# DeltaNet and a gated feed-forward on one core: two ways of inverting the first two pairs of chunks, and a new order of work

## The chip, the cores and the metric

The kernel runs on one core of one Trainium2 chip. That core has a matrix engine (TensorE, PE in the profile, its weight loads PEld), a vector engine (VectorE, DVE), a scalar engine (ScalarE, ACT), a general engine (GpSimd, POOL) and a synchronising engine (SyncE, SP); SP and ACT issue most of the DMA transfers, each in the order of its own instructions. The metric is the device time of one execution in microseconds; the median of several runs counts.

## The reference

```python
    batch, n_heads, seq, head_dim = (4, 8, 768, 48)
...
    k_n = k / (np.linalg.norm(k, axis=-1, keepdims=True) + 1e-06)
    state = np.zeros((B, H, D, D), dtype=np.float32)
    for t in range(S):
        kt, vt, bt = (k_n[:, :, t], v[:, :, t], beta[:, :, t, None])
        y[:, :, t] = np.einsum('bhd,bhde->bhe', q[:, :, t], state)
        v_old = np.einsum('bhde,bhd->bhe', state, kt)
        state = state + bt[:, :, :, None] * np.einsum('bhd,bhe->bhde', kt, vt - v_old)
...
    n_tokens, d_model, d_ff = (3072, 384, 2048)
...
    h = x @ w_in
    g = h * np.cos(h)
    return (g @ w_out).astype(np.float32)
```

The recurrence runs over 768 steps for 4 x 8 heads. Its outputs, turned to 3072 rows of 384, go through the feed-forward with the gate h cos(h). The weights arrive as 64-bit floats and are narrowed to 32 bits on the chip.

## The kernel before

**Units and pairs.** The 768 steps are cut into 24 chunks of C = 32, called units (n). A unit holds all 32 heads: 4 batches of 32 steps lie on the 128 partitions, 8 heads along the free dimension. Two units make a pair (m = n // 2), and a pair is also one block p of 256 tokens of the feed-forward.

**One unit.** Keys and queries are turned (`turn`, on PE for units 0 to 7, later by DVE), and `gram` multiplies keys by keys and by queries. `gram_keys` scales the key part by beta and the squared norm; it is I + N with N strictly triangular, 32 x 32 for each head. The unit needs its inverse. With it, `solve` turns the right side (v less what the state gives, `right_side`) into the updates u; `update` and `update_out` add them to the state; `through_state` and `within` give the outputs; `within_out`, `features` and `features_out` turn them into the columns x of the feed-forward. Units follow one another through the state.

**The inversion before.** For a pair the Gram blocks of both units are written to HBM (`gram_put`) and read back (`gram_get`) so that each partition holds one head's matrix. `invert` then eliminates column by column: for column j a product (L735) and a subtraction (L742), each on all 128 partitions. The result goes to HBM (`put`) and comes back as blocks (`get`). Pairs 1 to 11 do so on POOL with 31 columns, two partitions to a matrix. Pair 0 (HALVED = 1) inverts only the two diagonal 16 x 16 halves, on DVE: `fold` packs them, 15 columns are eliminated in PSUM, and the unit is then solved in two steps with the off-diagonal quarter between them (`solve_half`, `half_out`, `between`, `between_out`, `solve`).

**The feed-forward.** Pairs 0 and 1 are computed plainly (`hidden`, eight blocks p_h <- x_ffn, w_in a pair, at L951), the others with a Strassen-like scheme on PE (`layer`, L1125) whose sums are formed on DVE and POOL. The output of pair 0 is plain (`output`, L1148), those of the others use seven products (`product`, L1205). A gate takes an ACT pass, a DVE pass, the sine on ACT and a product on DVE. Each of the 28 weight tiles (12 of w_in, 16 of w_out) is loaded into a buffer of the gates, split by ACT (L495, L497), shifted by DVE (L501, L506) and added up by POOL (L510).

**The order.** Nothing is scheduled while it runs. Every piece of work is a task with a key; `Order.LINE` lists the tasks by number in the order in which they are written out, and each engine, and each DMA queue, keeps that order. `Order.OTHER` names the tasks that go to the second of two engines (POOL in place of DVE, ACT's queue in place of SP's). So an instruction that waits holds up everything behind it on its engine.

Of the kernel before, what the change touches and what calls it, by code (L numbers as in the profile page):

```python
# [10 lines left out]
FP = mybir.dt.float32  # L11
# [5 lines left out]
C = 32  # L17
DP = 64
SPLIT = 2
# [27 lines left out]

class Order:

    OTHER = {  # L50
        ('gram_put', 0), ('put', 0), ('get', 1), ('k', 2), ('gram_put', 2), ('q', 3), ('v',
        3), ('gram_get', 1), ('k', 5), ('k', 6), ('gram_put', 6), ('get', 6), ('v', 7),
        ('gram_put', 7), ('blocks', 8, 1), ('blocks', 9, 1), ('gram_put', 9), ('blocks', 11,
        1), ('put', 5), ('get', 11), ('blocks', 12, 1), ('gram_put', 12), ('blocks', 13, 1),
        ('put', 6), ('get', 14), ('put', 7), ('v', 16), ('blocks', 16, 0), ('get', 17),
        ('k', 18), ('v', 18), ('put', 9), ('k', 20), ('gram_get', 10), ('gram_put', 22),
        ('blocks', 23, 1), ('store', 0, 1), ('right', 4, 4), ('right', 3, 4), ('left', 1, 1,
        1), ('left', 1, 4, 0), ('in_sums', 20), ('x_sum', 2, 'd'), ('x_sum', 2, 'n'),
        ('x_sum', 2, 'm'), ('x_sum', 2, 'e'), ('x_sum', 2, 'k'), ('x_sum', 2, 'g'),
        ('x_sum', 2, 'l'), ('x_sum', 2, 'f'), ('left', 2, 1, 0), ('left', 2, 2, 0), ('left',  # L60
        2, 4, 0), ('store', 2, 0), ('x_sum', 3, 'd'), ('x_sum', 3, 'n'), ('x_sum', 3, 'e'),
        ('x_sum', 3, 'k'), ('x_sum', 3, 'g'), ('x_sum', 3, 'i'), ('x_sum', 3, 'l'),
        ('x_sum', 3, 'f'), ('x_sum', 3, 'h'), ('x_sum', 3, 'b0'), ('left', 3, 2, 0),
        ('left', 3, 3, 0), ('x_sum', 4, 'd'), ('x_sum', 4, 'n'), ('x_sum', 4, 'm'),
        ('x_sum', 4, 'e'), ('x_sum', 4, 'g'), ('x_sum', 4, 'f'), ('x_sum', 4, 'h'),
        ('x_sum', 4, 'b0'), ('left', 4, 1, 0), ('left', 4, 2, 0), ('left', 4, 1, 1),
        ('store', 4, 1), ('x_sum', 5, 'd'), ('x_sum', 5, 'n'), ('x_sum', 5, 'm'), ('x_sum',
        5, 'i'), ('x_sum', 5, 'l'), ('left', 5, 1, 0), ('left', 5, 2, 0), ('left', 5, 1, 1),
# [155 lines left out]
def kernel(  # L224
# [199 lines left out]
    for t in half_tiles:  # L424
        nc.vector.memset(t, 0.0)
        off_blocks.extend((t[:, 0], t[:, 1]))
        half_zt.extend((t[:, 2], t[:, 3]))
# [1353 lines left out]
```

## Time and profile before

| what | us |
|---|---|
| median of 3 runs (648.1 to 654.56) | 652.11 |
| the profiled execution | 653.98 |
| its span, first to last instruction | 652.2 |
| PE busy in it | 593.1 |
| DVE busy | 505.0 |
| POOL busy | 458.3 |
| ACT busy | 295.2 |
| first `hidden` block starts at | 71.2 |

The span is the profiled execution without what lies around it. In the page, the forty digits of an engine are its busy share in forty equal slices of 16.3 us, in tenths. A group of instructions is given by line, engine, operation and tiles, then its busy time, the mean of one in ns, and the idle time ahead of it with what ended it. The chain of waits is followed back from the last instruction: start, length, and what it was.

### The profile page before, as it was taken

To read this page: it belongs to the slowest core of one execution; us is meant where nothing else is said; L and a number is where in the kernel's file an instruction comes from. 1 tells how busy PE (TensorE), PEld (TensorE's weight loads), DVE (VectorE), ACT (ScalarE), POOL (GpSimd) and SP (SyncE) were. 2 spreads that over 40 slices of the span, in tenths; PEclk is the share of its full clock that TensorE was granted. 3 is DMA by queue.
4 is the path that set the end of the run, shared out by engine and by line. 5 is a ranking of instruction groups with operands and counts; after the bars stand their busy time and mean duration, and the time that the engine had idled before them with its cause. 6 is when DMAs were issued, how large, how long until landed. Compare 5 with 4: busy or idle time off the path is not lost.

```text
span 652.2 us, 23408 instructions
## 1 busy us (share of the span) xinstructions
PE 593.1 (91%) x9784; PEld 554.9 (85%) x9784; DVE 505.0 (77%) x1035; ACT 295.2 (45%) x518; POOL 458.3 (70%) x813
## 2 busy tenths in 40 slices
PE   3305789999999999999999999999999999999997
PEld 3204689897889999999999999999898999999997
DVE  4684498889879987988879879889668779666582
ACT  2534366663234444535634535536334545545340
POOL 4368878978898778888788787658687388424130
PEclk9999999999999999999999999999999999999999
DMA  8886576362473363454443622441531400300001
GB/s 167 199 183 158 135 179 145 88 135 46 66 122 58 53 112 59 86 82 73 85 74 52 113 42 54 56 88 22 100 69 24 82 12 3 58 2 25 1 24 26
DMA packets 215809, 51.52 MB, mean 79 GB/s; under 512 B 207256, under 2 KB 210600, under 8 KB 215704
## 3 DMA queue, kind: packets, MB, share of 16 engines
q1 hardware_dynamic: 160324, 35.06, 28.3%
q10 hardware_dynamic: 55124, 14.53, 11.0%
q8 instruction: 77, 1.26, 0.8%
q0 software_dynamic: 256, 0.45, 0.3%
q14 instruction: 28, 0.23, 0.1%
HBM read 39.24 MB, written 10.75 MB: 77 GB/s over the span
## 4 chain that ended last, share of the span: by engine, by line
PE 72%; POOL 8%; DMA 7%; DVE 5%; issue 3%; ACTq 2%; SPq 1%; ACT 1%; POOLq 0%; DVEq 0%
PE p_out L1205 25%; PE p_h L1125 23%; PE p_h L951 7%; POOL part L735 3%; POOL z L742 3%; PE p_out L1148 3%; PE p_kq L795 3%; DMA kp<-in_k_dram 3%; PE p_s L892 2%; PE p_kq L909 2%; PE p_u L867 2%; DMA gb<-g_dr 2%; PE p_g L625 1%; PE p_h L1205 1%; PE p_z L930 1%
## 5 line engine op out<-in xcount | busy, mean ns | idle before, releaser
L735 POOL TENSOR_TENSOR part<-z,gb 128x126 f32<-128x126 f32 (+22 forms) x341 | 150.8, 442 | 53.1 <-ACT g_ffn L1137 9.0
L742 POOL TENSOR_TENSOR z<-z,part 128x126 f32<-128x126 f32 (+22 forms) x341 | 155.1, 455 | 26.7
L1205 PE MATMUL p_out<-w_out,g_ffn 128*128 128x192 f32 x672 | 121.6, 329 | 2.9 <-ACT o L1244 1.5
L1205 PEld LDWEIGHTS p_out<-w_out,g_ffn 128*128 128x128 f32 x672 | 107.8, 190 | 4.3 <-ACT o L1244 1.7
L1004 ACT ACTIVATE turns<-turns,halfpi 128x512 f32<-128x512 f32 x96 | 68.3, 720 | 82.5 <-DVE turns L995 68.0
L1205 PE MATMUL p_out<-w_sum,g_ffn 128*128 128x192 f32 x496 | 90.8, 330 | 0.0
L1125 PE MATMUL p_h<-x_sum,w_in 128*128 128x128 f32 x640 | 83.3, 278 | 0.8 <-ACT p_h L1137 0.8
L1205 PEld LDWEIGHTS p_out<-w_sum,g_ffn 128*128 128x128 f32 x496 | 79.4, 190 | 1.2 <-DVE o L1257 0.2
L1125 PEld LDWEIGHTS p_h<-x_sum,w_in 128*128 128x128 f32 x640 | 77.5, 191 | 2.5 <-issue 0.6
L988 ACT ACTIVATE turns<-g_ffn,quarter_turn 128x512 int32<-128x512 f32 x70 | 49.6, 719 | 49.9 <-DVE g_ffn L1142 18.3
L1142 DVE TENSOR_TENSOR g_ffn<-g_ffn,p_h 128x512 f32<-128x512 f32 x80 | 54.0, 680 | 16.8 <-PE p_h L1125 15.5
L1007 DVE TENSOR_TENSOR g_ffn<-turns,g_ffn 128x512 f32<-128x512 f32 x70 | 51.7, 746 | 13.4 <-ACT turns L1004 13.2
L922 ACT COPY y<-p_kq 32x384 f32<-32x384 f32 x96 | 45.2, 470 | 34.4 <-PE p_kq L909 29.2
L995 DVE SCALAR_TENSOR_TENSOR turns<-g_ffn,turns 128x512 f32<-128x512 f32 x70 | 55.3, 798 | 6.2 <-ACT turns L988 6.2
L1125 PE MATMUL p_h<-x_sum,in_sum 128*128 128x128 f32 x400 | 53.7, 278 | 1.0 <-ACT p_h L1137 0.8
L1125 PEld LDWEIGHTS p_h<-x_sum,in_sum 128*128 128x128 f32 x400 | 49.7, 191 | 2.2 <-ACT p_h L1137 1.1
L951 PE MATMUL p_h<-x_ffn,w_in 128*128 128x128 f32 x384 | 48.2, 285 | 0.0
L1221 POOL TENSOR_TENSOR g_ffn<-g_ffn 128x512 f32<-128x512 f32 x21 | 30.3, 1450 | 24.8 <-DVE g_ffn L1007 14.6
L544 POOL TENSOR_TENSOR knrm<-ksum,halves 128x16 f32<-128x16 f32 (+1 forms) x14 | 37.9, 2711 | 12.8 <-DVE ksum L532 12.5
L951 PEld LDWEIGHTS p_h<-x_ffn,w_in 128*128 128x128 f32 x384 | 46.0, 199 | 1.1 <-POOL z L742 0.2
L1257 DVE SCALAR_TENSOR_TENSOR o<-p_out,o 128x192 f32<-128x192 f32 x74 | 25.0, 350 | 26.9 <-PE p_out L1205 26.0
L1125 PE MATMUL p_h<-x_ffn,w_in 128*128 128x128 f32 x320 | 42.3, 276 | 0.0
(135 smaller groups left out, 1018.8 us busy)
## 6 DMA issues: line engine op xcount, KB each, us to landing
gb<-g_dr SPq DMA_DIRECT2D x18, 256.0 KB
g_ffn<-in_moe_w_out_dram SPq DMA_DIRECT2D x11, 384.0 KB
vp<-in_v_dram SPq DMA_DIRECT2D x80, 48.0 KB
g_ffn<-in_moe_w_in_dram SPq DMA_DIRECT2D x6, 512.0 KB
g_ffn<-in_moe_w_in_dram ACTq DMA_DIRECT2D x6, 512.0 KB
kp<-in_k_dram SPq DMA_DIRECT2D x112, 24.0 KB
out_dram<-o SPq DMA_DIRECT2D x13, 192.0 KB
zt<-z_dr SPq DMA_DIRECT2D x72, 32.0 KB
```

What stands on the lines that cost most here:

```text
L544: nc.gpsimd.tensor_tensor(out=scales[m][2][:, part], in0=sums[m, part.start][:, 0:n], in1=halves[:, 0:n], op=ALU.pow,)
L735: eng.tensor_tensor(out=part, in0=z[:, 0:rows, j, None].to_broadcast(shape), in1=a[:, j, None, j + 1 :].to_broadcast(shape), op=ALU.mult,)
L742: eng.tensor_tensor(out=behind, in0=behind, in1=part, op=ALU.subtract)
L922: nc.scalar.copy(by_parity(y[quarter(b)]), p_kq[quarter(b ^ 1), :, b % 2])
L951: nc.tensor.matmul(p_h[:, i], w_in[:, t, (4 * k + i) * 128 : (4 * k + i + 1) * 128], xts[p][:, t, unit * 128 : (unit + 1) * 128], start=(i ...
L988: nc.scalar.activation(turns[p, f], hidden_of(p, f), AF.Identity, bias=quarter_turn, scale=TURN)
L995: nc.vector.scalar_tensor_tensor(out=r, in0=hidden_of(p, f), scalar=TURN, in1=t, op0=ALU.mult, op1=ALU.subtract,)
L1004: nc.scalar.activation(r, r, AF.Sin, bias=halfpi, scale=2.0 * math.pi)
L1007: nc.vector.tensor_tensor(out=place(p, f), in0=step_of(rests.pop((p, f)), f), in1=step_of(hidden_of(p, f), f), op=ALU.mult,)
L1125: nc.tensor.matmul(p_h[:, e], in_block(*w)[:, e], x_of(p, b), start=new and e == 0, stop=True, skip_group_check=True,)
L1142: nc.vector.tensor_tensor(out=part_of(p, to), in0=part_of(p, one), in1=part_of(p, two), op=op)
L1205: nc.tensor.matmul(p_o, left(p, part, a)[:, e % 4], right(e, b), start=(e == 0), stop=(e == FT // 2 - 1), skip_group_check=True,)
```

## The change

Pair 0 is no longer inverted by elimination. For its two units (DOUBLED = 2) the inverse is formed on PE by doubling, unit by unit, without a trip to HBM. Of I + N the two diagonal 16 x 16 blocks are taken with a mask. With the powers N^2, N^4, N^8 the inverse of a diagonal block is (I - N)(I + N^2)(I + N^4)(I + N^8); two more products add the off-diagonal quarter. That is six levels; a level is done for even and odd heads apart (`par`), 16 matmuls of 32 x 32 blocks each. PE needs each power in both orientations: DVE turns 32 x 32 blocks, ACT copies the other one, DVE adds. The twelve matrices of 8 x 32 columns of a unit lie in buffers that are free until later: unit 0's in `in_sum`, unit 1's in `w_sum`. The sums that are to fill those buffers now wait until units 0 to 3 are solved. `solve` then uses the whole inverse in 32-row blocks.

The half-column scheme moves from pair 0 to pair 1 (`m == HALVED` in place of `m < HALVED`): its trips to HBM carry 16 columns in place of 32, its elimination has 15 columns in place of 31, and units 2 and 3 are solved in two steps. It runs on POOL in four parts; the first part (`('inv', 1, 0)`, four columns) is given to DVE. The clearing of the half tiles moves from DVE to POOL (`half_tiles`), and a small constant (the masks) is loaded by POOL ahead of beta.

LINE and OTHER are new throughout: of the 28 weight loads SP's queue carries 25 in place of 17 (ACT's 3 in place of 11), the loads of units 0 to 5 stand on SP's queue with a weight load after every four transfers, and 11 sums of x go from DVE to POOL while 6 sums of gates go the other way. The lists are left out here.

```diff
+    DOUBLED, HALVED, HC = 2, 1, C // 2
...
+    def power(n):
+        whole = (in_sum, w_sum)[n].rearrange("p a b c -> p (a b c)")
+        return whole[:, 0 : POWERS * H * C].rearrange("p (x h i) -> p x h i", h=H, i=C)
+
+    N_T, N1, P2, P2_T, Y0, P4, P4_T, Y1, P8, Y2, Y3, OFF = range(POWERS)
+    Y3_T, MIX_T, WHOLE = N_T, N1, Y0
+
+    def masked(n, x, mask):
+        nc.vector.tensor_tensor(
+            out=power(n)[:, x], in0=gs[n], in1=mask[:, None, :].to_broadcast([128, H, C]),
+            op=ALU.mult,
+        )
+
+    def double_first(n):
+        masked(n, N_T, near_block)
+        m = power(n)
+        nc.vector.transpose(m[:, N1], m[:, N_T])
+
+    def double_rest(n):
+        m = power(n)
+        nc.vector.tensor_tensor(
+            out=m[:, Y0], in0=eye32[:, None, :].to_broadcast([128, H, C]), in1=m[:, N_T],
+            op=ALU.subtract,
+        )
+        masked(n, OFF, far_block)
+        gs.pop(n)
+
+    LEVELS = [
+        (N1, slice(N_T, N_T + 1)), (P2, slice(P2_T, Y0 + 1)), (P4, slice(P4_T, Y1 + 1)),
+        (P8, slice(Y2, Y2 + 1)), (OFF, slice(Y3_T, Y3_T + 1)), (MIX_T, slice(Y3, Y3 + 1)),
+    ]
+    COPIES = {0: P2_T, 1: P4_T, 4: MIX_T}
+    TURNS = {0: P2, 1: P4, 2: P8}
+    ADDS = {1: (Y1, Y0, 1), 2: (Y2, Y1, 1), 3: (Y3, Y2, 0), 5: (WHOLE, Y3, 0)}
+
+    def double(n, level, par):
+        m = power(n)
+        p = p_ds[n, par] = h_bank("p_d", n, level, par).rearrange(
+            "p x (j i) -> p x j i", i=C
+        )
+        one, two = LEVELS[level]
+        for j in range(NP):
+            for b in range(B):
+                nc.tensor.matmul(
+                    p[quarter(b), 0 : two.stop - two.start, j],
+                    m[quarter(b), one, 2 * j + par],
+                    m[quarter(b), two, 2 * j + par],
+                )
...
-        eng = nc.gpsimd if tag is None else nc.vector
+        eng = either(("inv", m, x), nc.gpsimd, nc.vector)
         for j in columns:
-            rows, last = j // SPLIT + 1, C
-            if m < HALVED:
-                rows, last = j + 1, HC
+            rows, last = (j + 1, HC) if m == HALVED else (j // SPLIT + 1, C)
...
-        zt, rhs = zts.pop(n), rhss.pop(n)
+        zt, rhs = power(n)[:, WHOLE] if n < DOUBLED else zts.pop(n), rhss.pop(n)
...
-                if n < 2 * HALVED:
+                if n < DOUBLED or n // 2 == HALVED:
                     for b in range(B):
...
                 if x == 1:
-                    deps = deps + [("solve", 1), ("beta_home",)]
+                    deps = deps + [("solve", n) for n in range(4)] + [("beta_home",)]
...
             if len(to) == 2:
                 deps.append(plain_done)
+            else:
+                deps += [("solve", n) for n in range(4)]
```

More of the change, by code (lines that the diff above doesn't have):

```diff
@@ L54 @@
[L54 to L65, printed above, removed]
```

257 lines of the change are left out of this document (148 added, 109 removed), and 195 rows, old and new, of tables (LINE, OTHER).

## The prediction

> **What bounds the kernel now.** I read the busy totals and the forty slices of the page first, then a table by stage, then the chain of waits, and last the groups and the timelines of single engines in the opening stretch.
>
> ```profile
> PE 593.1 (91%) x9784; PEld 554.9 (85%) x9784; DVE 505.0 (77%) x1035; ACT 295.2 (45%) x518; POOL 458.3 (70%) x813
> PE   3305789999999999999999999999999999999997
> ```
>
> TensorE (PE) is busy 593.1 of 652.2 us, and the slices say where it isn't: in the first six. The stages, cut where the first feed-forward block starts (71.2), show the same in us:
>
> ```profile
> 0.00:71.20 71.20, 26.61 (x715) 21.54 (x715) 44.14 (x123) 28.27 (x52) 42.77 (x62) 1.00 0.78 175
> 71.20:100.00 28.80, 24.56 (x582) 23.07 (x578) 20.41 (x38) 16.86 (x33) 22.41 (x40) 1.00 0.67 163
> 100.00:600.00 500.00, 495.08 (x8172) 464.05 (x8172) 412.91 (x831) 236.11 (x413) 380.98 (x704) 1.00 0.37 67
> 600.00:652.20 52.20, 46.86 (x324) 46.19 (x322) 27.51 (x45) 13.96 (x22) 12.14 (x9) 1.00 0.06 16
> ```
>
> Columns: stretch, its length, busy PE, weight load, DVE (VectorE), ACT, POOL, then clock, DMA share, GB/s. PE idles 44.6 us before 71.2, 4.2 until 100, 4.9 in the next 500 and 5.3 at the end. So the time is (start of the first feed-forward block) + (566.5 us of PE work from there) + (14.5 us of later idling) = 652.2. Only the first term is large enough to be worth an edit. The chain of waits says what it is made of; these are its long links:
>
> ```profile
> 11.26 3.29 POOL knrm L544 x2
> 19.70 4.67 DMA g_dr<-g
> 24.97 2.51 DMA gb<-g_dr
> 35.44 1.36 ACTq L374
> 37.79 3.95 DMA kp<-in_k_dram
> 43.90 1.76 issue
> 45.66 4.05 DMA gb<-g_dr
> 61.40 2.63 DMA qp<-in_q_dram
> 68.27 1.89 PE p_kq L795 x64
> 70.16 1.11 PE p_g L625 x61
> 71.27 4.89 PE p_h L951 x24
> ```
>
> The reader is to see that before 71 us the chain hardly touches TensorE: the Gram blocks go to HBM (19.70) and come back in another layout (24.97), VectorE then eliminates column by column, and the result makes the same trip before unit 0 can be solved.
>
> **The new start.** For pair 0 the change removes the trip out and back, 30 elimination steps on DVE, two folds and two half solves. It adds 384 small matmuls in 24 blocks (2 units, 6 levels, 2 parities), 12 copies on ACT, and on DVE 8 operations on 256 columns and 32 on 128. In the new instruction order DVE must get through everything up to the copy of the first state before the state product, the Gram block and the first feed-forward block can run. I cost that stretch from the groups of DVE before 71.2:
>
> ```profile
> L501 DVE SCALAR_TENSOR_TENSOR g_ffn<-g_ffn 128x512 uint32<-128x512 uint32 (+1 forms) x12 | 8.8, 733 | 9.7 <-ACT g_ffn L497 9.7
> L506 DVE TENSOR_SCALAR w_in<-w_in 128x512 uint32<-128x512 uint32 x11 | 7.3, 666 | 0.0
> L742 DVE TENSOR_TENSOR p_h<-p_h,w_sum 128x15 f32<-128x15 f32 (+7 forms) x15 | 3.2, 213 | 0.5
> L532 DVE TENSOR_REDUCE ksum<-g_ffn 128x8 f32<-128x384 f32 (+1 forms) x5 | 3.0, 626 | 5.7 <-ACT g_ffn L527 5.7
> L636 DVE TENSOR_TENSOR g<-p_g,bs 128x256 f32<-128x256 f32 x4 | 1.7, 416 | 0.0
> L879 DVE TENSOR_TENSOR u<-p_u,bz 128x384 f32<-128x384 f32 x2 | 1.0, 552 | 0.7 <-PE p_u L861 0.7
> L449 DVE STREAM_TRANSPOSE w_sum<-w_sum 128x768 f32<-128x768 f32 x1 | 1.0, 967 | 0.0
> L902 DVE COPY st<-p_s 128x768 f32<-128x768 f32 x1 | 0.9, 944 | 0.0
> L648 DVE TENSOR_SCALAR g<-g,consts 128x128 f32<-128x128 f32 x2 | 0.6, 278 | 0.0
> ```
>
> - 8 weight conversions at 0.733 + 0.666: 11.2
> - 5 sums of squares at 0.626: 3.1
> - 8 Gram products at 0.416: 3.3
> - 8 doubling operations on 256 columns at the same 0.416: 3.3
> - 30 doubling operations on 128 columns (2 of the 32 come later). The trace has no such operation; the bounds are 0.213 (a PSUM operation on at most 64 columns) and 0.278 (one on 128 columns out of SBUF). I take 0.278, the same width: 8.3; the other end gives 6.4
> - the transpose of beta 0.97, the weighing of v and the state copy 0.94 each (768 columns), scaled values 1.1, two folds of three operations at about 0.3 (1.8), 8 elimination operations of pair 1 at 0.21 (1.7): 7.5
> - four key scalings of five small operations, estimated at 0.21 each like L742: 4.3
>
> The sum is 41.0 (39.1 at the low end). DVE can start on data at about 9 us; now its first reduction stands at
>
> ```profile
> 10.62 0.56 DVE ksum L532
> ```
>
> because ACT issued a key load ahead of the square that feeds it, and that load moves to SP's queue. Then 9 + 41 = 50, plus 1.89 and 1.11 from the chain (L795, L625): the first feed-forward block would start at 53. Rows of back-to-back operations overlap (the chain counts this reduction with 0.56, its group with 0.626): at 0.07 for about 100 operations that is 7 us in favour, and 46 is the near end. The far end is a DVE that waits as it does now: 9.7 us of idle time stood before L501 alone, which gives 63. The overlap is certain and some waiting is too; **I take 51**, nearer to the end that the operations' own rows make.
>
> Two things lie beside this. The 24 PE blocks are half of an L825 product each:
>
> ```profile
> 53.46 1.90 PE L825 MATMUL p_w<-vp,w_sum 32*32 32x48 f32 x64 [3.86 <-ACT kq_t L602]
> ```
> ```profile
> 76.10 0.88 PE L825 MATMUL p_w<-rhs,w_sum 32*32 32x48 f32 x64
> 77.63 0.88 PE L825 MATMUL p_v<-g_ffn,w_sum 32*32 32x48 f32 x64 [0.65 <-ACT g_ffn L837]
> ...
> 94.52 2.84 PE L951 MATMUL p_h<-x_ffn,w_in 128*128 128x128 f32 x24
> 97.30 1.15 PE L867 MATMUL p_u<-rhs,zt 64*64 64x48 f32 x32
> ```
>
> The same 64 instructions take 1.90 us in the sparse opening and 0.88 later, with the granted clock at 1.00 in both. So 24 blocks cost 24 x 0.95 = 22.8 or 24 x 0.44 = 10.6 us, in 44.6 us of idle PE. The first feed-forward block pays too: 4.89 in the chain against 2.84. I leave all at the slow price. [...] ACT's 12 copies (under 0.4 us each, 4.8) fall into an engine that is busy 28.3 of 71.2 us. If their cover went, they would add to the levels one by one.
>
> **Work after the start.** Half-column solving moves from units 0 and 1 to units 2 and 3. Before, one unit of it (two products, 0.85 each) lay behind 71.2; now two do: +1.7. Units 2 and 3 then solve with 32-row blocks (0.88) in place of L867 (1.15): -0.5. Sum +1.2. Later idling stays 14.5: pair 1 now stalls PE in place of the 4.2 us between 71.2 and 100. Its Gram blocks are fetched by ACT, which waits there for their write; behind that wait are the first outputs and features of unit 0, and on DVE the eight elimination columns stand before the state copy. By the same DVE sum its folds end at 34 to 37 (9 us, plus 5 of the conversions, 18 of the 128-column operations and all that stands before them); 4.67 + 2.51 for the trip (chain) put the data there at 41 to 44, while DVE still has some 10 us of work ahead of them. 51 + 566.5 + 1.2 + 14.5 = **633**.
>
> **The second supply.** POOL must not be late with pair 2:
>
> ```profile
> L742 POOL TENSOR_TENSOR z<-z,part 128x126 f32<-128x126 f32 (+22 forms) x31 | 12.7, 411 | 2.4
> L735 POOL TENSOR_TENSOR part<-z,gb 128x126 f32<-128x126 f32 (+22 forms) x31 | 11.7, 377 | 2.2
> ```
>
> That is pair 1's whole inversion (50 to 84 us): 29.0 with its gaps. Now POOL does 22 steps of at most 64 elements, some 0.36 each with the gap: 8, plus memsets of about 1.4. It is freed of 19.6 us:
>
> ```profile
> 97.27 0.34 POOL L735 TENSOR_TENSOR part<-z,gb 128x31 f32<-128x31 f32 x1
> ```
> ```profile
> L510 POOL TENSOR_TENSOR w_out<-w_out,g_ffn 128x384 uint32<-128x384 uint32 x9 | 9.3, 1054 | 0.1
> ```
> ```profile
> 146.69 2.75 PE L1148 MATMUL p_out<-w_out,g_ffn 128*128 128x384 f32 x8
> 149.37 1.14 PE L867 MATMUL p_u<-rhs,zt 64*64 64x48 f32 x32
> ```
>
> Pair 2's inversion, which started at 97.3 and led to the solve of unit 4 at 149.4, may start at 77 or earlier. Of nine weight additions among its steps three are left (6 x 1.05), so the solve comes about 46 us after the start: at 123, or 118 if POOL waits less for DVE as well. The new order puts three hidden blocks and one output (3 x 2.78 + 2.68 = 11.0, from the starts of the rows) behind that solve which stood before it, so the old time for the same point is 149.4 - 11.0 = 138.4. A solve at 118 to 123 is then 15 to 20 us earlier, less the 1.2: 633 to 638, the same size by another road. The remaining moves (11 sums of inputs from DVE to POOL, 6 sums of gates the other way) change DVE by +1 us and POOL by -2 in 650: nothing. The sums of w_in now wait until units 0 to 3 are solved, because the powers live in their buffer: 22 operations on 512 columns, under 0.94 each, 21 us at most, for which the plain blocks of pairs 0 and 1 still ahead are the cover (over 20 blocks of about 2.7). If that cover fails, the first Strassen products wait for them one by one.
>
> The profiled run's time is 653.98 with a span of 652.2; the median of the runs shown is 652.11, so span and median may be equated. **Forecast 634**, between the two sums; its own range 622 to 641.
>
> **Rivals.**
> - *Smaller gain.* DVE keeps waiting on converted weights as now (9.7 us before L501). Weights move from 17 to 25 loads on SP's queue, so a load that waits for its buffer holds up the keys behind it. The first block starts at 61, the end is 643. For: DMA share 0.78 in the stretch. Against: the bytes and the 16 engines are the same, and fewer Gram blocks travel.
> - *No change.* The level hand-offs aren't hidden. Two units of six levels, each 0.95 on PE and 0.65 until PE gets the copied result (77.63), are 19 us if nothing overlaps. On top of 51 that is 70, and the end 652. Against: two parities and two units are interleaved in the order.
> - *Slower.* Pair 2's Gram fetch stands on SP behind pair 1's results and the w_out loads. Each us of its delay past the PE's arrival costs one us, and the 11 us of plain work that now stand behind unit 4's solve make it worse: the time is 652.2 + 1.2 + (start + 46 - 138.4). It breaks even at a start of 91; at 100 it gives 661. For it: most of the w_out loads wait in that queue for buffers. Against: POOL would need to be later than now with 20 us less to do.
>
> **Chances.** Forecast 0.62, smaller gain 0.21, no change 0.09, slower 0.08. A per cent (6.5 us) is what a measurement of this kernel can tell from no change. The range 622 to 648 takes in the forecast's own and the smaller gain, and leaves out about 0.2: the gains beyond 30 us and the two last rivals. Faster by over 1% is 0.62 + 0.21 = 0.83, within 1% 0.09, slower 0.08.
>
> **What would show it.** Right: the first block of hidden (p_h from x_ffn) starts near 51, no DMA of Gram blocks for pair 0 in the chain, POOL's first full inversion starts at 72 to 78. Wrong: a first block past 60, DVE idle time before the doubling's transposes, or PE waiting for zt at the solve of unit 4.

## The result, and the profile after

The changed kernel takes 649.1 us (median of 20 runs, 646.87 to 651.54) against 653.06 us for the kernel before (20 runs, 648.1 to 658.79); the ratio is 0.995, 95% interval 0.9932 to 0.9967. It is faster by half a per cent, where 634 us had been forecast, 3%. The profiled execution took 650.1 us, its span is 648.3.

The page of the changed kernel: busy totals, two of its rows of forty slices, and one of its DMA queues (packets, MB, share of 16 engines).

```profile
PE 611.4 (94%) x10616; PEld 571.5 (88%) x10616; DVE 514.8 (79%) x1046; ACT 296.1 (46%) x528; POOL 434.6 (67%) x782
...
PE   4768779999999999999999999999999999999997
...
PEclk9955979999999999999999999999999999999999
...
q8 instruction: 83, 1.36, 0.9%
```

The opening is no longer empty: slices 2 to 6 have PE at 6 to 8 tenths. But in the slices from 32 to 65 us, and again near 81 to 97, the granted clock is at 5 to 7 tenths. That row alone doesn't tell a slow PE from a fast one: in the kernel before the state product ahead of the first block took 1.96 us and the block itself 4.96 with the clock row at 1.00, here 1.96 and 5.75 with 0.50. The table by stage, cut at the first feed-forward block, which now starts at 60.61 (before: 71.20; forecast: 51):

```profile
0.00:60.61 60.61, 39.71 (x1355) 33.41 (x1355) 45.27 (x130) 28.90 (x60) 32.33 (x47) 0.76 0.85 197
60.61:100.00 39.39, 31.38 (x831) 28.93 (x827) 29.27 (x57) 20.25 (x40) 26.27 (x41) 0.84 0.54 127
100.00:600.00 500.00, 497.36 (x8151) 466.78 (x8150) 412.64 (x815) 234.52 (x409) 365.37 (x688) 1.00 0.37 65
600.00:648.30 48.30, 42.98 (x288) 42.38 (x286) 27.65 (x46) 12.38 (x19) 10.63 (x8) 0.98 0.06 17
```

Columns as before: stretch, length, busy PE, weight load, DVE, ACT, POOL, then clock, DMA share, GB/s. The same sum as in the prediction: 60.6 (start) + 571.7 (PE work from there, 611.43 - 39.71) + 16.0 (idle PE: 8.0, 2.6 and 5.3 in the three later rows) = 648.3. Forecast was 51 + 567.7 + 14.5. So of the 15 us that are missing, 9.6 are in the start, 4.0 in PE's work and 1.5 in its idle time.

The chain of waits of the opening (start, length, what), with the links that stand where g_dr, gb and late queries stood before:

```profile
12.69 5.09 DMA kp<-in_k_dram
...
29.82 1.37 issue
...
37.89 1.12 DVE g L726
...
39.03 1.27 DVE g L727
...
44.12 1.51 DVE w_in L512
...
51.41 1.21 DVE z L808
...
55.62 0.90 PE p_z L987 x3
56.52 0.58 PE p_h L693 x32
57.10 1.89 PE p_kq L852 x64
58.99 0.58 PE p_h L693 x32
59.57 1.11 PE p_g L631 x61
```

No trip of Gram blocks is left in it. There is a late key load; a time in which PE waits for nothing that the profile shows ("issue"); and VectorE operations far too long for their size. L726, on 128x128, takes 1.1 us here; the same form took 0.28 in the kernel before. VectorE and GpSimd side by side, around that place (start, length, instruction):

```profile
35.56 0.43 DVE L642 TENSOR_TENSOR g<-p_g,bs 128x256 f32<-128x256 f32 x1 [0.24 <-PE p_g L631]
35.90 0.30 DVE L705 STREAM_TRANSPOSE in_sum<-in_sum 128x128 f32<-128x128 f32 x1
36.12 1.10 DVE L507 SCALAR_TENSOR_TENSOR g_ffn<-g_ffn 128x512 uint32<-128x512 uint32 x1
...
37.81 1.18 DVE L726 TENSOR_SCALAR g<-g,consts 128x128 f32<-128x128 f32 x1
39.03 1.27 DVE L727 SCALAR_TENSOR_TENSOR g<-g,consts 128x128 f32<-128x128 f32 x1
...
40.43 0.27 DVE L726 TENSOR_SCALAR g<-g,consts 128x128 f32<-128x128 f32 x1
40.73 0.35 DVE L727 SCALAR_TENSOR_TENSOR g<-g,consts 128x128 f32<-128x128 f32 x1
```
```profile
35.39 1.28 POOL L516 TENSOR_TENSOR w_in<-w_in,g_ffn 128x512 uint32<-128x512 uint32 x1 [11.29 <-DMA qp<-in_q_dram]
37.64 2.52 POOL L516 TENSOR_TENSOR w_in<-w_in,g_ffn 128x512 uint32<-128x512 uint32 x2 [0.97 <-DVE w_in L512]
```

GpSimd adds two weight blocks from 37.64 to 40.16. VectorE's L726 and L727 on unit 3, started in that time, end at 38.99 and 40.30; the same two on unit 2, after it, take 0.27 and 0.35. The product with a PSUM operand (35.56) and the 32x32 turn (35.90) run beside an addition and are not held. Seven operations before 55 us are held like this (1.30, 1.10, 1.18, 1.27, 1.46, 1.51 and 1.20 us, against 0.17, 0.68, 0.27, 0.35, 0.69, 0.42 and 0.18 elsewhere), 6.3 us in all. L726 and L727 each end 0.1 us after an addition does (the first of the two ends at 38.92, the second at 40.16); what decides whether an operation is held, no row shows. The prediction had no term for it.

Later, TensorE:

```profile
79.72 0.88 PE L882 MATMUL p_v<-g_ffn,in_sum 32*32 32x48 f32 x64 [0.61 <-ACT g_ffn L894]
84.03 1.11 PE L598 MATMUL p_t<-consts,kp 128*128 128x128 f32 x4 [3.43 <-DVE g_ffn L902]
84.93 1.06 PE L598 MATMUL p_t<-consts,qp 128*128 128x128 f32 x4
85.79 4.91 PE L1008 MATMUL p_h<-x_ffn,w_in 128*128 128x128 f32 x24
...
91.44 2.94 PE L1008 MATMUL p_h<-x_ffn,w_in 128*128 128x128 f32 x24
```

PE waits 3.43 us for the difference for p_v (L902), which stands on VectorE behind weight conversions that GpSimd's additions hold up. In the chain of waits the last of them (L512, 0.41 us when it is not held) and the difference stand directly ahead of the turns:

```profile
82.36 1.15 DVE w_in L512
83.51 0.47 DVE g_ffn L902
84.03 1.97 PE p_t L598 x8
```

After that wait the two turns and the feed-forward block run at half pace (4.91 us; the next one takes 2.94). So three suspects stood before the experiments, called theories 1 to 3 in what was expected of them: the additions, the place of L902 in the order, and PE's slow pace. A fourth, PE's supply with its own instructions beside the traffic of the weights, came out of them.

### The profile page after: what moved, and what is told of

The parts are those of the page before. It is cut to its first block, busy times and chain, and to the rows that moved or that the text cites. A ratio compares the mean times of both kernels' runs of the same rounds, so it can differ in the third digit from the quotient of the medians.

```text
span 648.3 us, 25034 instructions
## 1 busy us (share of the span) xinstructions
PE 611.4 (94%) x10616; PEld 571.5 (88%) x10616; DVE 514.8 (79%) x1046; ACT 296.1 (46%) x528; POOL 434.6 (67%) x782
## 3 DMA queue, kind: packets, MB, share of 16 engines
q8 instruction: 83, 1.36, 0.9%
## 4 chain that ended last, share of the span: by engine, by line
PE 81%; DVE 8%; DMA 3%; ACT 2%; SPq 2%; issue 2%; DVEq 0%; ACTq 0%
PE p_out L1262 27%; PE p_h L1182 25%; PE p_h L1008 8%; PE p_kq L852 3%; PE p_out L1205 3%; PE p_g L631 3%; PE p_s L949 2%; PE p_kq L966 2%; DMA kp<-in_k_dram 2%; PE p_u L924 2%; DVE g_ffn L1064 1%; PE p_z L987 1%; SPq L385 1%; PE p_t L598 1%; PE p_h L1262 1%
## 5 line engine op out<-in xcount | busy, mean ns | idle before, releaser
L801 POOL TENSOR_TENSOR part<-z,gb 128x126 f32<-128x126 f32 (+23 forms) x321 | 142.6, 444 | 46.8 <-ACT z L789 9.3
L808 POOL TENSOR_TENSOR z<-z,part 128x126 f32<-128x126 f32 (+23 forms) x321 | 142.7, 445 | 25.2
L1064 DVE TENSOR_TENSOR g_ffn<-turns,g_ffn 128x512 f32<-128x512 f32 x70 | 58.2, 839 | 6.6 <-ACT turns L1061 6.5
L1052 DVE SCALAR_TENSOR_TENSOR turns<-g_ffn,turns 128x512 f32<-128x512 f32 x70 | 54.1, 782 | 10.6 <-ACT turns L1045 10.5
L1008 PE MATMUL p_h<-x_ffn,w_in 128*128 128x128 f32 x384 | 51.2, 295 | 0.0
L1008 PEld LDWEIGHTS p_h<-x_ffn,w_in 128*128 128x128 f32 x384 | 48.8, 208 | 1.2 <-issue 0.2
L1278 POOL TENSOR_TENSOR g_ffn<-g_ffn,g_ffn 128x512 f32<-128x512 f32 x15 | 20.3, 1354 | 39.2 <-PE p_out L1262 21.6
L1182 PE MATMUL p_h<-x_ffn,w_in 128*128 128x128 f32 x320 | 42.6, 276 | 0.0
```

Source lines behind the costliest of these rows:

```text
L801: eng.tensor_tensor(out=part, in0=z[:, 0:rows, j, None].to_broadcast(shape), in1=a[:, j, None, j + 1 :].to_broadcast(shape), op=ALU.mult,)
L808: eng.tensor_tensor(out=behind, in0=behind, in1=part, op=ALU.subtract)
L1008: nc.tensor.matmul(p_h[:, i], w_in[:, t, (4 * k + i) * 128 : (4 * k + i + 1) * 128], xts[p][:, t, unit * 128 : (unit + 1) * 128], start=(i ...
L1052: nc.vector.scalar_tensor_tensor(out=r, in0=hidden_of(p, f), scalar=TURN, in1=t, op0=ALU.mult, op1=ALU.subtract,)
L1064: nc.vector.tensor_tensor(out=place(p, f), in0=step_of(rests.pop((p, f)), f), in1=step_of(hidden_of(p, f), f), op=ALU.mult,)
L1182: nc.tensor.matmul(p_h[:, e], in_block(*w)[:, e], x_of(p, b), start=new and e == 0, stop=True, skip_group_check=True,)
```

## The experiments

Each kernel starts from the changed one unless it is said otherwise. "Start" is the start of the first feed-forward block in the profiled execution. or_on_dve, or_and_diff and half_page have the same opening but for a us, and start at 59.3, 57.2 and 59.2: a difference of one or two us between single executions is no result. The time scatters too: the 20 runs of the changed kernel spread over 4.7 us.

**or_on_dve and or_on_dve_old.** The addition becomes an OR in VectorE's shift, in the changed kernel and in the kernel before.

```diff
-        nc.vector.tensor_scalar(w, w, 3, None, op0=ALU.logical_shift_left)
+        nc.vector.scalar_tensor_tensor(
+            out=w, in0=w, scalar=3, in1=lo,
+            op0=ALU.logical_shift_left, op1=ALU.bitwise_or,
+        )
...
-        nc.gpsimd.tensor_tensor(out=w, in0=w, in1=words.pop(t)[:, :, 0], op=ALU.add)
+        words.pop(t)
```

> The changed kernel, but the last step of each weight conversion (GpSimd's 32-bit addition of the low bits, 24 of them at 1.0 to 1.4 us) is done by VectorE in its shift: (w << 3) | low in one operation of 0.68 instead of a shift of 0.41. An OR in place of an addition differs in the last bits of a weight where the rounded low bits carry. Theory 1 (VectorE's operations are held up while a GpSimd addition runs: seven of them before 55 us took 1.10 to 1.51 us instead of 0.17 to 0.69, 6.3 us in all, and five conversions ahead of the difference for p_v took 4 us too long): the long operations vanish, VectorE pays 8 x 0.27 = 2.2 more by then, the first feed-forward block starts at 55 to 57 instead of 60.6, PE's 3.43 us wait at 80.6 shrinks to under 1 and the block after it runs at 2.9 instead of 4.9; 638 to 642 us. Rival (TensorE at its slow pace and the hand-offs set the start): first block at 59 or later, 646 or more.

Measured: 646.47 us, ratio to the kernel before 0.9898 (0.9855 to 0.994); start 59.3. VectorE in the same place:

```profile
38.67 0.28 DVE L728 TENSOR_SCALAR g<-g,consts 128x128 f32<-128x128 f32 x1
38.98 0.35 DVE L729 SCALAR_TENSOR_TENSOR g<-g,consts 128x128 f32<-128x128 f32 x1
```

Both folds at their own length: the additions were what held VectorE, that much is shown. PE's wait for p_v's difference fell to 0.96 and the block behind it to 2.84. But the start moved by 1.3 and not by 4 to 5. Up to the end of the copy of the first state VectorE was busy 36.0 us in place of 39.1, but idle 9.0 in place of 7.0: most of what it saved it then waited. PE shows a wait of a new kind:

```profile
32.92 0.64 PE L633 MATMUL p_g<-kq_t 48*32 48x64 f32 x20 [0.71 <-DVE tt L739]
35.51 0.93 PE L633 MATMUL p_g<-kq_t 48*32 48x64 f32 x44 [1.95 <-issue]
```

PE stops for 1.95 us after 20 of the 64 products of one Gram block, with nothing to wait for that the profile shows. Five such stops before the start make 6.4 us in this run; the changed kernel has three, 2.1 us; the kernel before has none. That they took the place of the held operations is not shown: diff_first below, whose opening is that of the changed kernel, has 6.3 us of them and starts at 59.8.

> The same edit in the kernel before. Theory 1: the trips over HBM, not VectorE, set its start (before: 71.2), so it moves by 2 us at most: 649 to 652 us, and the changed order is what made the additions costly. Rival (the additions cost both kernels the same): start at 66, 646 or less.

Measured: 652.11 us, ratio 0.9974 (0.9944 to 1.0003); start 68.6. The kernel before gains 0.3% by it, with no change still in the interval. The start moved by 2.6, a little over the bound of theory 1 and short of its rival's 66; the time is at the end of the range of theory 1. The start moved no less than in the changed kernel (1.3), so it is not shown that the new order made the additions costly.

**diff_first.** One task moves in the order.

```diff
+    MOVES = [(('between_out', 2), ('between', 2))]
...
+        for key, behind in self.MOVES:
+            line.remove(key)
+            line.insert(line.index(behind) + 1, key)
```

> The changed kernel with one move in the order: the difference for unit 2 (the operation that reads p_v) stands right behind its product, ahead of the last weight conversions. Theory 2 (an in-order VectorE made PE wait 3.43 us, and the wait cost PE its fast pace): PE's wait at 80.6 falls under 1 us, the next block takes 2.9 instead of 4.9 us, the two turns 0.6 each instead of 1.1; 643 to 646 us. Rival (the time comes back before 100 us, since the moved conversions are late): 648 or more.

Measured: 645.63 us, ratio 0.9881 (0.9853 to 0.9909); start 59.8.

```profile
80.85 0.66 PE L605 MATMUL p_t<-consts,kp 128*128 128x128 f32 x4 [0.73 <-DVE g_ffn L909]
81.34 0.60 PE L605 MATMUL p_t<-consts,qp 128*128 128x128 f32 x4
81.78 2.84 PE L1015 MATMUL p_h<-x_ffn,w_in 128*128 128x128 f32 x24
```

The wait is 0.73 in place of 3.43, the turns take 0.66 and 0.60, the block 2.84: as theory 2 said, in size too (645.6 in 643 to 646). One instruction behind the wrong neighbours cost the changed kernel about as much as its whole measured gain.

**warm_pe.** Unused products in the opening, behind each of PE's tasks.

```diff
+            if opening and key[0] in self.ON_PE:
+                self.warm(8 if key == ("turn", 0) else 4)
...
+            nc.tensor.matmul(p_out[:, 0, 0:128], ident, ident)
```

> The changed kernel with unused products added on PE: in the opening, four of 128x128 on 128 columns (eight at the start) behind each PE task up to the first feed-forward block, some 110 in all. Theory 3 (PE's slow pace before 66 us sets the start): if they bring PE to its fast pace, a doubling block of 32 products of 32 columns takes 0.33 instead of 0.65, a state product 1.15 instead of 1.96, the first feed-forward block starts at 55 to 57 and takes 2.9 instead of 5.75; 640 to 644 us. Theory 1 (VectorE sets the start): start at 59 to 61, the block itself 2.9; 645 to 647. If they don't bring it to the fast pace, they only stand in the way: start at 64 to 70, 652 or more.

Measured: 660.35 us, ratio 1.0093 (1.0059 to 1.0127); start 75.5. PE by groups, from 9 to 72.5 us (busy, mean ns, idle before):

```profile
L1820 PE MATMUL p_out<-consts 128*128 128x128 f32 x308 | 44.2, 288 | 0.0
L700 PE MATMUL p_h<-in_sum 32*32 32x32 f32 x256 | 3.6, 194 | 0.0
```

The unused products brought PE to its fast pace (a doubling product 194 ns where the changed kernel has 238, a block of 32 in 0.45 us in place of 0.65) and stood in the way for 44 us. The expectation had counted some 110 products; the trace has 308 (each product of the code shows as two: the 32 that half_page, below, adds are 64 in its trace). What the fast pace alone would be worth stays open. One row of use: before the fifth block PE waited 2.54 us, and the turns and the block after it were slow again (1.12 and 4.84 us).

**light_weights_or and light_weights.** Seven eighths of the weights' traffic are taken away; the output misses most of the feed-forward weights.

```diff
-        queue("weights", t).dma_start(out=words[t], in_=src)
+        few = 2 * n // 8
+        queue("weights", t).dma_start(out=words[t][:, 0:few], in_=src[:, 0:few])
...
```

> or_on_dve, with only an eighth of each weight block loaded (the rest of the staging tiles is cleared once at the start, so most of the feed-forward weights are zero); every operation stays, the load traffic of the opening falls by some 5.5 MB. Theory 4 (what took the place of the held-up VectorE is PE's own instruction supply: PE stands with nothing to wait for in the middle of blocks, 6.4 us before the first feed-forward block, against none in the kernel before; it fetches its instructions over the same DMA engines that the weights keep busy): these stops shrink to 2 us or less, start at 52 to 55 instead of 59.3; 636 to 641 us. Rival 4b (the supply is slow by itself, a page of 256 instructions every 3.5 us at best, whatever else is moved): the stops stay at 5 us or more and the start at 57 to 59.

> The changed kernel with the same light loads and GpSimd's additions kept. Theory 1 plus 4: VectorE's long operations (1.1 to 1.5 us) are still there beside each addition, PE's stops without a cause fall under 1 us; start at 55 to 58 instead of 60.6. If the weights' traffic were the whole reason, it would start as early as light_weights_or; if traffic plays no part, at 60 to 61.

Measured, one time each: 635.85 and 640.99 us. The table by stage, up to the start, of light_weights_or and of light_weights:

```profile
0.00:52.82 52.82, 33.40 (x1355) 28.41 (x1355) 45.42 (x134) 28.95 (x60) 24.34 (x41) 0.87 0.57 101
```
```profile
0.00:55.40 55.40, 35.48 (x1356) 29.97 (x1356) 48.74 (x134) 29.09 (x60) 35.95 (x51) 0.81 0.55 98
```

This pair says most. With most of the traffic (0.85 of the DMA engines busy in the changed kernel, 0.57 and 0.55 here) and the additions both away, the start is 52.8 and the time 635.9, near the forecast's 51 and 634. The additions put back cost 2.6 us of start and 5.1 of span (634.1 to 639.2); the traffic put back costs 5.2 of start and 9.1 of span (639.2 to 648.3). Both together are far outside the scatter, and so is the traffic by itself; the part of the additions, between two single executions, is not. That the weights are mostly zero plays no part: from the start on PE worked 568.7 us in light_weights_or, and 568.3 in or_and_diff below, which has the full weights. PE's stops were 2.3 and 0.6 us, a little over theory 4's figure in the first, within it in the second.

**or_and_diff.** Both edits together.

> or_on_dve and diff_first together. Either alone removed PE's wait at 80.6 us, so together they should not add up: the start is that of or_on_dve (57 to 60), the wait is gone; 643 to 647 us. If the two gains were separate, 638 to 640.

Measured: 645.31 us (640.19 to 647.06), ratio 0.987 (0.9825 to 0.9915); start 57.2, in the fastest of the five executions. The gains don't add up: PE's wait at 80 us is one thing with two remedies. It beats the kernel before and the changed one, but it cannot be told from either edit alone.

**extra_page and half_page.** Unused small products on PE: 128 in the middle of the opening, or 64 ahead of all work.

```diff
...
+        for i in range(32):
+            at = quarter(i % 4)
+            nc.tensor.matmul(p_out[at, 0, 0:1], ident[at, 0:32], ident[at, 0:1])
```

> or_on_dve with 64 unused products of 32x32 on one column put on PE behind the turn of unit 2 (128 products in the trace, 256 instructions, about 1.5 to 2.6 us of PE time by the rate of the doubling blocks). Theory 4 and 4b: one page of instructions more, 3.5 us or more later, 62 to 64 instead of 59.3, with more time in PE's stops. Rival (VectorE or the hand-offs set the start, PE's supply has slack): start at 59 to 61.

Measured: 648.58 us once, start 64.4. That is just past the range of theory 4 (62 to 64), but it says little: all 128 products went to one corner of the array and took 6.9 us by themselves (in half_page 64, spread over four, take 1.0), and PE's stops were 2.7 us, where or_on_dve had 6.4. The size of a page can't be read from it.

> or_on_dve with 32 unused products of 32x32 on one column, spread over PE's four row and column groups, put ahead of PE's first turn (64 products in the trace, 1 to 2 us, while PE still waits for data). Theory 4 (PE stands where a page of its instructions ends): counted from the kernel's first product, the stops without a cause lie near 218, 343, 469, 596, 724, 850, 977, 1105 as in all runs so far, so each falls 64 products earlier in the code, in other blocks than before (none 20 products into the Gram block of unit 3, where two kernels stopped at 596). Rival (the stops belong to certain operations): they stay in their blocks, at counts 64 higher. The start moves by 1 to 2 us either way.

Measured: 648.55 us once, start 59.2. The places where PE stops:

```profile
37.09 0.79 PE L697 MATMUL p_h<-in_sum 32*32 32x32 f32 x42 [0.26 <-issue]
...
45.20 0.41 PE L922 MATMUL p_u<-vp,in_sum 32*32 32x48 f32 x19 [0.62 <-issue]
...
49.20 1.21 PE L953 MATMUL p_s<-u,kp 64*64 64x96 f32 x22 [0.95 <-issue]
```

Counted from the first product by the x of each row, these stops lie after 725, 978 and 1106 products. In or_on_dve the stops at 724 and 977 were in doubling blocks and the one at 1105 in a product for p_kq; here the same counts fall in another doubling block, in the solve and in the state's update, and there they are. Over the thirteen kernels with the new order, 44 stops before the first feed-forward block lie at nine counts only: 218, 343 to 345, 469, 596, 724 or 725, 852, 977 or 978, 1105 or 1106, and 1233, that is 125 to 128 products apart. The profile gives the rest: queue q8, of kind "instruction", moved 83 packets, 1.36 MB in all, 16 KB each; 10616 products and as many weight loads, shared out over them, are 256 instructions a packet, 128 products with their weights (in the kernel before 9784 and 77 packets, 254). That fits the distance between stops, so a stop is taken here for PE at the end of such a packet of its own instructions (a page of instructions from here on); that it waits there for the next one to land is the likely reading, no row shows one landing. Before its first feed-forward block the changed kernel runs 1355 products, ten pages, in 60 us; the kernel before 715 in 71. A stop takes 0.17 to 3.07 us. The 3.5 us a page in what was expected of light_weights_or and extra_page was the author's estimate; in half_page the counts 852 and 978 lie 2.5 us apart (42.0 to 44.6).

The start of half_page is that of or_on_dve with 1.8 us of stops in place of 6.4. diff_first had 6.3 us of them, the changed kernel 2.1 with the same opening and a start 0.8 us later. So the stops are there, but their sum doesn't set the start by itself.

**late_conversions.** or_and_diff, with weight blocks 4 to 17 converted behind the first feed-forward block, and the loads from block 8 on later.

```diff
+        (('weights', 8), ('weights', 11)),
...
+        (('shift', 4), ('double_add', 1, 5, 1)),
+        (('shift', 5), ('shift', 4)),
+        (('shift', 6), ('solve_out', 1)),
+        (('shift', 7), ('update_out', 1)),
...
```

> or_and_diff with a new place for the weight conversions: the first feed-forward block reads only the first three weight blocks, yet nine were converted ahead of it. Blocks 4 to 17 are converted behind it (each ahead of the block that needs it), and their loads from block 8 on are issued later. If VectorE's sum and the weights' traffic set the start (theories 1 and 4), five conversions of 1.36 us less stand ahead of it and PE's stops shrink: start at 50 to 54, 637 to 642 us. If the chain of PE's own products and stops sets it, start at 57 or later and 644 or more; if the moved conversions now make the second or third feed-forward block late, the start is early but PE idles over 8 us from there to 100 us, and the time is 643 to 647.

Measured: 657.39 us, ratio 1.0044 (1.002 to 1.0067); start 58.9. The table by stage, before and behind the start:

```profile
9.00:58.85 49.85, 33.74 (x1347) 28.53 (x1348) 33.33 (x109) 25.62 (x55) 16.95 (x31) 0.78 0.76 178
58.85:100.00 41.15, 25.55 (x589) 23.73 (x585) 28.94 (x57) 17.31 (x35) 9.09 (x16) 0.79 0.57 139
```

VectorE had 33.3 us of work in that stretch where or_and_diff had 39.6, and the start came no earlier. With the traffic there, VectorE's sum alone doesn't set it: the sum theory falls in this form. Start and time lie where the second case had them (57 or later, 644 or more). But the extra time came by the third case's road: PE idled 15.6 us from there to 100 (41.15 - 25.55; 5.4 in or_and_diff), waiting among others for copies of ACT, and that cost more than the 643 to 647 expected for it.

**one_doubling.** or_and_diff without the doubling of unit 1, which is solved with unit 0's inverse.

```diff
+            if key[0].startswith("double") and key[1] == 1:
+                emit = lambda: None
...
-        zt, rhs = power(n)[:, WHOLE] if n < DOUBLED else zts.pop(n), rhss.pop(n)
+        zt, rhs = power(0)[:, WHOLE] if n < DOUBLED else zts.pop(n), rhss.pop(n)
```

> or_and_diff with the whole doubling of unit 1 left out (unit 1 is solved with the inverse of unit 0): 384 products in the trace (three pages of PE's instructions) and 18 operations of VectorE, some 5.3 us, none of which the first feed-forward block reads. The prediction's step (doubling lies hidden in idle PE, VectorE's sum sets the start): the start moves by VectorE's 5 us at most and, since late_conversions took as much from VectorE without moving it, rather not at all: 55 to 58. Theory 4 (PE's products and pages are the path in the opening): three pages and 12 blocks of 0.65 us, some 8 to 11 us, leave it: 47 to 51.

Measured: 643.81 us once, start 54.6, between the two expectations and nearer to the first: 384 products and 18 operations of VectorE gone, 2.6 us gained. That is hardly more than two executions of one opening differ by, and the time lies within those of or_and_diff (640.19 to 647.06): the doubling of one unit is mostly hidden, whether wholly is open. ACT now waits 8.0 us for weight blocks (1.9 in or_and_diff).

**traffic_aside and keys_first.** How does the traffic act? The first, from light_weights_or, puts it back on ACT's queue into an unused buffer, the second (from or_and_diff) moves the first weight loads behind the keys of pair 1.

```diff
+            nc.scalar.dma_start(out=rest[:, at : at + 2 * n - few], in_=src[:, few:])
```
```diff
+        (('weights', 0), ('k', 3)),
+        (('weights', 1), ('q', 2)),
+        (('weights', 2), ('q', 3)),
...
```

> light_weights_or with the traffic put back where nothing waits for it: behind each of the first 12 light loads, ACT's queue loads the other seven eighths of that block into a buffer that is not used before the first feed-forward block (12 loads of 448 KB, 5.4 MB). Theory 4 (the traffic itself slows the key loads and PE's pages of instructions): the start goes back from 52.8 to 57 to 60, with PE's stops at 4 us or more. Rival (the light blocks helped because they free SP's queue and the staging buffers sooner, so keys and conversions come earlier): the start stays at 52 to 55, stops at 2 us.

Measured: 647.88 us once, start 63.9, stops 2.0 us: later than either case, and theory 4's longer stops (4 us or more) did not come. ACT waited 5.9 us for keys (2.3 in light_weights_or), so the traffic makes keys late where no staging buffer and no place on SP's queue hang on it. But part of the start is the experiment's own: ACT also stood 3.2 us on one of the added loads, and in the chain of waits two of them take 6.6 us (2.99 at 31.10, 3.60 at 41.64). An estimate without these, 57.3, would still be outside the rival's 52 to 55; that makes the rival unlikely and doesn't rule it out.

> or_and_diff with the loads of the keys and queries of units 2 and 3 issued ahead of the first three weight blocks instead of between them (only the order of loads on SP's queue changes). If the weights' traffic acts by making the early keys late (the second key load of pair 1 lands at 16.8 us and ACT's copy of unit 1 waits behind its square), the key lands 2 to 3 us earlier and the start moves from 57.2 to 54 to 55; 641 to 643 us. If it acts on everything at once (pages, staging, keys alike), the keys' gain is lost to later weight blocks: start at 56.5 to 59.5, no difference that can be measured (644 to 647). If the weights are the narrowest supply, the start is later, 60 or more.

Measured: 649.88 us, ratio 0.995 (0.9919 to 0.998); start 66.4, the third case.

```profile
ACT w_in L513 <- DMA g_ffn<-in_moe_w_in_dram: 7.8, 2, 6.2
ACT kq_t L622 <- PE p_t L612: 6.8, 3, 5.1
```

The first weight block, moved by two key loads, came so late that ACT stood 6.2 us before its conversion, and behind that stood the copy of a turned unit that PE needed. So here, with the DMA engines at 0.77 from 9 us to the start, keys put ahead made a weight block late, and with it everything behind its conversion on ACT.

## Why the prediction was wrong

The sign was right and the size was not: 649.1 against 634, outside the range (622 to 648).

*The new start, 51.* This is the step that failed: "I take 51, nearer to the end that the operations' own rows make." Measured 60.6. Its terms can be measured one by one, with the stretch cut as the prediction cut it, at VectorE's first reduction and at the end of the copy of the first state:

```profile
54.03 0.92 DVE L959 COPY st<-p_s 128x768 f32<-128x768 f32 x1
```

| us | first reduction at | VectorE busy from there to the end of the copy | VectorE idle in it | from there to the start | start |
|---|---|---|---|---|---|
| forecast, by its rows | 9 | 41.0 | none | 3.0 | 53, taken as 51 |
| changed kernel | 8.8 | 39.1 | 7.0 | 5.7 | 60.6 |
| light_weights | 8.8 | 38.9 | 2.1 | 5.6 | 55.4 |
| light_weights_or | 9.1 | 35.3 | 3.0 | 5.3 | 52.8 |
| late_conversions | 8.9 | 30.8 | 11.4 | 7.8 | 58.9 |

Three terms of the step were wrong. First, waits within the operations: the busy time came out near the sum, but 6.3 us of it are operations held by additions, which the sum did not have; without them 32.8 are left of the 41.0, about the 7 us less that the near end had for overlapping rows. Second, waits between the operations: 7.0 us, where the prediction set waits and overlap off against each other at 2 us in its favour. Third, what follows the copy: 5.7 in place of 3.0. The sum took only the state product and the Gram block (1.89 and 1.11). On the chain stand also the product p_z (0.90) and two blocks of unit 1's doubling (0.58 each). p_z stood there in the kernel before too:

```profile
67.39 0.88 PE p_z L930 x3
```

The far end of the step, 63, had been "a DVE that waits as it does now", 9.7 us before L501. That wait is 0.9 us in the changed kernel, so the far end came near the truth by other waits: luck.

Both kinds of waits could have been suspected from the trace of before. The same operation came in two lengths there, and its mean of 666 ns was quoted without asking why. VectorE in the kernel before, two of its shifts:

```profile
39.07 0.42 DVE L506 TENSOR_SCALAR w_in<-w_in 128x512 uint32<-128x512 uint32 x1
40.01 1.50 DVE L506 TENSOR_SCALAR w_in<-w_in 128x512 uint32<-128x512 uint32 x1
```

GpSimd added from 39.62 to 41.22. The mean of such a group holds the waits of the conversions, so these came out right (0.808 and 0.549 after, 10.9 for eight, against 11.2). But folds, scaled values and elimination steps were priced at their clean length, and in the new order they stand beside additions too: 4.0 of the 6.3 us fell on them. The other sign was the DMA share of 0.78 in that stretch, cited only under a rival. Between light_weights and the changed kernel it is VectorE's idle time that grows, by 5.0 of the 5.2 us that the traffic costs; between the two light runs it is the busy time, by 3.6, of which 2.6 reach the start. With both away the start is 52.8, near the 51, but not by the forecast's terms: less VectorE work than its sum, and more behind the copy. Nor is VectorE's sum the bound by itself: late_conversions took 6 us out of it with the traffic there; VectorE's idle time and what follows the copy grew instead (11.4 and 7.8 us, against 7.5 and 5.0 in or_and_diff), and nothing moved.

*24 blocks on PE, hidden.* They took 18.1 us of PE (4.3 + 4.1 + 5.0 + 4.7 in its groups up to the start), between the two prices of 22.8 and 10.6. Hidden was mostly right: 4.4 us of them stand on the chain of waits up to the start, and half of them, with their VectorE operations, cost about 2.6 us of start by one_doubling's single execution, hardly more than the scatter. What the step lacked is that products are instructions: nearly twice as many products ahead of the start (1355 for 715) are nearly twice the pages, and PE stops at the ends of some (2.1 us in the changed kernel, none before); what that costs the start is not shown. Nor did the doubling make PE faster behind it: PE was busy without a break from 56.5 us, and the first block still took 5.75 us (4.96 before), with a granted clock of 0.50 in its first 3.4 us.

*Work after the start, +1.2.* Measured +5.2 (566.5 to 571.7), 4.0 more than forecast. The slow pace is most of the difference: 2.1 in the block at 85.79 (4.91 for 2.84), 0.9 in the two turns before it, 0.8 in the first block. The prediction counted idle time and work apart and had no term for slower work behind an idle time.

*Idling unchanged, 14.5.* Measured 16.0, 3.43 of it one wait. The prediction named pair 1 as the staller and priced it at 4.2, but did not ask what stood ahead of `between_out` on VectorE in the new order. diff_first shows that this place alone was worth some 3.5 us.

*The second supply.* Wrong in its start and without effect. GpSimd's first full inversion began at 87.5, not 72 to 78: the Gram block of unit 5 ran only at 73.3, and its trip came behind. But it was done at 121, and PE took the solve of unit 4 at 137.2 with no wait:

```profile
87.50 0.24 POOL L801 TENSOR_TENSOR part<-z,gb 128x31 f32<-128x31 f32 x1
```
```profile
137.20 1.14 PE L924 MATMUL p_u<-rhs,zt 64*64 64x48 f32 x32
```

So the second sum, "the same size by another road" (633 to 638), was no second witness: by then PE's own work set the time, and PE came to the solve at 137.2, 1.2 us ahead of the old equivalent of 138.4.

*The trips.* Right. No Gram trip of pair 0 is left, and pair 1's trip is hidden behind VectorE's work; the cover is thin, since VectorE waits 2.2 us for it in one_doubling.

*The rivals.* "Smaller gain" had the start at 61, as it came, and the loads as its reason, which came in part: the traffic costs 5.2 us, and SP's loads of keys, queries and values waited 5.3 us on weight loads; but VectorE no longer waits on converted weights (0.9 us for 9.7), and the additions it did not have. Its 643 lacked the slow pace and the wait at 80 us. "No change" (652) came nearer in size than the forecast, for a reason that did not hold (hand-offs between levels that nothing hides). "Slower" needed pair 2's inversion to start after 91; it started at 87.5.

What stays open is how the traffic takes its 5 us. It shows as VectorE's idle time; late keys, late weight blocks and PE's pages all appear in the waits, in other shares in each execution, and no run here separates them.

## What to carry to other kernels

Before adding up an engine's operations into a new start, ask of each mean why it is so long: here a shift of 1.50 us, where another of its size took 0.42, told of a neighbour, and that neighbour was there after the change too. In an opening in which several engines and the loads wait for one another in order, a step off one engine's sum need not be a step off the time (late_conversions took 6 us off VectorE's, and the start came 1.7 later than in or_and_diff); price the waits as a term of their own, and take two suspects away together and put them back one at a time. A rewritten order must be read line by line at the few tasks that PE waits for: one of them, behind weight conversions, gave back as much as the change gained.

## What the runs showed of the hardware

- Beside GpSimd's 32-bit additions (128x512, 1.28 us) VectorE's folds took 1.18 us in place of 0.27 (L726) and 1.27 in place of 0.35 (L727); without the additions, in or_on_dve, 0.28 and 0.35. A product with a PSUM operand and a 32x32 turn ran on (0.43 and 0.30 beside an addition). The other way too: an addition that started beside a VectorE product of 768 columns took 2.08 us in place of 1.28.
- A DMA queue of kind "instruction" (q8, 0.9% of the 16 engines' time) moved 83 packets of 16 KB for PE's 10616 products and as many weight loads, 256 a packet. In the openings of the new order, with small products following closely, PE stops for 0.2 to 3.1 us at counts 125 to 128 products apart, also with the engines at 0.55 (light_weights, one stop of 0.60); the kernel before, with half the products in its opening and the engines at 0.78, has no stop there. From 100 to 600 us, where 24 products take 2.8 us, all of PE's idle time is 2.6 us.
- After waits of 2.54 and 3.43 us PE ran at half pace for the next turns and one block (4.84 and 4.91 us for 2.84). The length of the wait alone doesn't decide: after 0.96 us in or_on_dve the turns and the block ran fast (0.66, 0.60 and 2.84), after 0.95 in light_weights_or slow (1.10, 1.06 and 3.67). In the opening of the changed kernel it ran at that pace for 9.8 us without a break (56.45 to 66.3), so being busy was not enough there.
